# Strided sparse attention and an ELU layer: the first pair's q and k transposed as fp32, the first quarter of w_in in two loads, and a new order

## The chip, the cores and the metric

One core of a Trainium2 chip runs the whole program. The metric is the device time of one execution in microseconds. The engines are TensorE (PE; its weight loads are shown as PEld), VectorE (DVE), ScalarE (ACT), GpSimd (POOL) and SyncE (SP). Each takes its instructions in the order in which the program issues them and waits on semaphores for the others. Loads that also convert fp32 to bf16 are issued from POOL's queue; plain copies and stores from the queues of SP and ACT.

## The reference

Attention over 8 batches of 8 heads, 576 tokens of 64 features; heads 0 to 3 are local, heads 4 to 7 strided. Its result, 4608 tokens by 512 features, goes through two layers with an ELU between them.

```python
scores = scale * np.matmul(q, k.transpose(0, 1, 3, 2))
rel = pos[:, None] - pos[None, :]
mask_local = (rel >= 0) & (rel < stride)                      # stride = 32
mask_strided = (rel >= 0) & (pos[None, :] % stride == pos[:, None] % stride)
scores = np.where(masks, scores, -1e9)
attn = softmax(scores)
x = (attn @ v) as 4608 x 512
h = x @ w_in                                                  # 512 x 2048
g = np.where(h > 0.0, h, np.exp(np.minimum(h, 0.0)) - 1.0)
out = g @ w_out                                               # 2048 x 512
```

## The kernel before

Heads go in pairs. A key such as 0s1 names batch 0, strided heads, second pair; 0l0 the first local pair. A pair passes through these steps, each written as a token with a letter: T (transposes of q or k on PE, for batches 0 and 1 only; later batches use transposing DMAs, X), c or C (the copy of a transpose out of PSUM, on DVE or ACT), S (scores, L453), e (exponential on ACT, L460), m (mask on DVE, L467 and L473), O (the products with v and the row sums, L480 to L501), n and r (Ln and Exp, by which ACT takes the reciprocal of the sums, L551 and L556), x (the scaling on DVE that writes xT, L581). Most steps come in two halves.

The layers work on nine chunks of 512 tokens. The first layer makes 16 tiles of 128 hidden features for a chunk, four matmuls of 512 columns each (L608); two of the four read the strided half of xT, two the local half. For chunk 0 the halves are separate tokens, a (strided) and b (local); later chunks use L for all four. Then h (exponential, ACT), i or j (clamp on DVE, L625, or ACT, L623), g (maximum, DVE). The second layer, Z (L642), adds up 16 matmuls for each of four groups of 128 tokens; q or o copies the result out (L648, DVE or ACT) and t or u stores it. The last group is cut into pieces, Y and y (L672, L682).

The order of all this is written out by hand in the string ORDER, some 1400 tokens that are run one after another; a token's last digits name the PSUM banks. The order of one engine's instructions is that of the tokens. D tokens are loads on POOL's queue. W (L588) copies v of a strided batch into its layout, V (L585) moves rows of a local batch, and F fills constants. w tokens are filler: matmuls on a tile of zeros (L385) that write to a bank nobody reads yet.

The loads of POOL's queue share eight semaphores, so that the ninth in flight waits for the landing of the first.

For pair 0s0 the kernel doesn't use a converting load. Ahead of ORDER, SP loads q and ACT loads k of its two heads as fp32 into `stage`, each in two halves (L297). The tokens K and k cast the halves to bf16 (L390, on ACT or DVE), and T with a part number transposes four blocks of 72x128 (L401), whose copies are at L421. Heads 0s1 arrive as bf16 by two loads on POOL.

Of the kernel before, what the change touches and what calls it, by code (L numbers as in the profile page):

```python
# [8 lines left out]
F32 = mybir.dt.float32  # L9
BF16 = mybir.dt.bfloat16  # L10
I32 = mybir.dt.int32
ALU = mybir.AluOpType
# [35 lines left out]
C.1s0.q i.0.4 a.0.13.6 h.0.6 g.0.4 a.0.14.5 b.0.12 a.0.15.2 h.0.12 b.0.15 j.0.6 D.vs.1 a.0.2.1 j.0.12
b.0.13 g.0.6 b.0.2 h.0.13 g.0.12 a.0.1.4 h.0.2 i.0.7 b.0.1 i.0.13 a.0.3.3 g.0.7 h.0.1 D.wo3.0 b.0.3
i.0.2 b.0.14 h.0.3 g.0.2 a.0.0.7 j.0.1 b.0.0 a.0.11.1 g.0.1 h.0.0 a.0.10.0 h.0.14 D.vl.1 i.0.0 b.0.10  # L50
j.0.3 g.0.0 b.0.11 h.0.10 a.0.8.4 g.0.3 b.0.8 h.0.11 g.0.13 Z.0.0.0.7 h.0.15 i.0.10 D.ks.2 i.0.14
Z.0.0.1.7 h.0.8 g.0.10 j.0.11 Z.0.3.0.6 j.0.15 g.0.11 D.vs.2 Z.0.3.1.6 g.0.15 g.0.14 a.0.9.3 D.qs.2
i.0.8 b.0.9 g.0.8 Z.0.1.0.5 h.0.9 j.0.9 T.1s0.k.4 D.kl.2 Z.0.1.1.5 C.1s0.k g.0.9 T.1s1.k.2 S.1s0.1.01
c.1s1.k T.1l1.k.4 e.1s0.1 T.1l1.q.3 c.1l1.k T.1l0.q.2 S.1s1.0.01 m.1s0.1 Z.0.3.2.6 e.1s1.0 C.1l1.q
m.1s1.0 Z.0.1.2.5 C.1l0.q O.1s1.0.43 T.1l0.k.2 n.1s1.0 S.1s1.1.01 c.1l0.k Z.0.0.2.7 e.1s1.1 r.1s1.0
S.1s0.0.01 S.1l1.1.23 x.1s1.0 e.1s0.0 Z.0.1.3.5 m.1s1.1 m.1s0.0 e.1l1.1 Z.0.0.3.7 q.0.1 m.1l1.1 D.kl.3
S.1l0.1.01 S.1l1.0.23 V.1 e.1l0.1 Z.0.3.3.6 q.0.0 e.1l1.0 O.1l1.1.54 X.ks.2 m.1l1.0 O.1s0.1.73 n.1l1.1
m.1l0.1 S.1l0.0.01 n.1s0.1 Z.0.2.0.2 q.0.3 r.1l1.1 r.1s0.1 x.1l1.1 e.1l0.0 O.1s0.0.64 x.1s0.1 O.1l1.0.53
W.2 n.1s0.0 O.1l0.1.71 n.1l1.0 Z.0.2.1.2 m.1l0.0 r.1s0.0 X.qs.2 n.1l0.1 x.1s0.0 r.1l1.0 D.ql.2
O.1s1.1.04 r.1l0.1 x.1l1.0 O.1l0.0.63 n.1s1.1 x.1l0.1 Z.0.2.2.2 n.1l0.0 r.1s1.1 r.1l0.0 Z.0.2.3.2  # L60
x.1s1.1 X.kl.2 x.1l0.0 L.1.12.7 t.0.1 L.1.6.6 h.1.12 i.1.12 L.1.3.5 h.1.6 D.ks.3 i.1.6 L.1.4.4 h.1.3
D.vl.2 g.1.6 L.1.1.3 g.1.12 h.1.4 i.1.3 L.1.5.6 h.1.1 g.1.3 D.vs.3 L.1.13.7 i.1.4 h.1.5 i.1.1 i.1.5
L.1.0.5 h.1.13 g.1.5 D.qs.3 o.0.2 L.1.7.1 g.1.1 j.1.13 D.ql.3 g.1.4 h.1.0 L.1.2.6 X.ql.2 h.1.7 g.1.13
L.1.10.0 j.1.0 i.1.7 h.1.2 g.1.7 L.1.14.7 t.0.2 h.1.10 g.1.0 j.1.2 S.2s1.0.12 S.2s1.1.34 i.1.10 t.0.0
L.1.8.5 g.1.2 e.2s1.1 e.2s1.0 g.1.10 L.1.15.6 t.0.3 h.1.8 m.2s1.1 m.2s1.0 h.1.14 S.2s0.0.01 S.2s0.1.23
X.ks.3 L.1.9.4 e.2s0.1 i.1.14 g.1.14 h.1.15 L.1.11.3 e.2s0.0 i.1.15 h.1.9 Z.1.3.0.7 g.1.15 h.1.11 i.1.8
Z.1.3.1.7 j.1.9 g.1.8 m.2s0.1 O.2s1.1.01 Z.1.2.0.2 i.1.11 n.2s1.1 g.1.9 O.2s0.1.56 r.2s1.1 g.1.11
Z.1.2.1.2 n.2s0.1 x.2s1.1 Z.1.3.2.7 r.2s0.1 m.2s0.0 O.2s1.0.01 x.2s0.1 Z.1.2.2.2 n.2s1.0 O.2s0.0.34
r.2s1.0 Z.1.3.3.7 n.2s0.0 x.2s1.0 Z.1.2.3.2 r.2s0.0 q.1.3 S.2l0.0.01 S.2l0.1.56 x.2s0.0 Z.1.1.0.7
e.2l0.0 q.1.2 e.2l0.1 m.2l0.0 S.2l1.0.01 S.2l1.1.34 X.qs.3 Z.1.1.1.7 m.2l0.1 e.2l1.0 e.2l1.1 m.2l1.0  # L70
O.2l0.0.56 O.2l0.1.01 X.kl.3 n.2l0.0 m.2l1.1 Z.1.0.0.4 n.2l0.1 Z.1.0.1.4 r.2l0.0 t.1.3 O.2l1.1.23
r.2l0.1 x.2l0.0 Z.1.0.2.4 n.2l1.1 x.2l0.1 O.2l1.0.56 r.2l1.1 Z.1.0.3.4 X.ql.3 n.2l1.0 x.2l1.1 Z.1.1.2.7
r.2l1.0 D.qs.4 Z.1.1.3.7 x.2l1.0 D.kl.4 q.1.0 L.2.11.6 W.3 S.3s0.0.01 S.3s0.1.23 h.2.11 L.2.3.5 e.3s0.1
i.2.11 g.2.11 L.2.7.4 D.ks.4 h.2.3 o.1.1 D.vl.3 i.2.3 L.2.2.6 m.3s0.1 e.3s0.0 g.2.3 L.2.5.7 h.2.7 h.2.2
i.2.7 L.2.4.5 h.2.5 g.2.7 j.2.2 i.2.5 L.2.9.3 m.3s0.0 h.2.4 D.vs.4 g.2.5 L.2.0.4 h.2.9 g.2.2 j.2.4
D.ql.4 L.2.14.7 i.2.9 h.2.0 g.2.4 O.3s0.1.01 h.2.14 g.2.9 L.2.10.6 n.3s0.1 i.2.0 L.2.6.5 i.2.14 h.2.10
g.2.0 r.3s0.1 L.2.8.3 i.2.10 X.ks.4 g.2.14 h.2.6 L.2.13.4 x.3s0.1 h.2.8 j.2.6 g.2.10 O.3s0.0.01 X.qs.4
L.2.1.7 n.3s0.0 i.2.8 g.2.6 L.2.15.6 r.3s0.0 g.2.8 t.1.0 h.2.1 L.2.12.5 x.3s0.0 h.2.15 X.kl.4 i.2.1
S.3s1.0.01 S.3s1.1.23 g.2.1 e.3s1.1 Z.2.1.0.7 e.3s1.0 m.3s1.1 i.2.15 h.2.13 m.3s1.0 S.3l0.0.01
S.3l0.1.23 h.2.12 g.2.15 Z.2.1.1.7 e.3l0.1 i.2.12 j.2.13 Z.2.1.2.7 g.2.12 e.3l0.0 g.2.13 O.3s1.1.23  # L80
S.3l1.0.01 S.3l1.1.56 m.3l0.1 n.3s1.1 Z.2.1.3.7 m.3l0.0 e.3l1.1 Z.2.0.0.4 e.3l1.0 m.3l1.1 r.3s1.1
m.3l1.0 O.3s1.0.01 q.2.1 O.3l1.1.56 Z.2.0.1.4 n.3l1.1 x.3s1.1 t.2.1 n.3s1.0 Z.2.3.0.7 r.3l1.1 X.ql.4
O.3l1.0.23 Z.2.0.2.4 r.3s1.0 x.3l1.1 n.3l1.0 x.3s1.0 Z.2.3.1.7 t.1.2 r.3l1.0 S.4s1.0.01 S.4s1.1.56
x.3l1.0 t.1.1 Z.2.0.3.4 e.4s1.1 e.4s1.0 m.4s1.1 O.3l0.1.23 O.3l0.0.56 q.2.0 n.3l0.1 Z.2.3.2.7 W.4
r.3l0.1 Z.2.2.0.4 m.4s1.0 D.vs.5 n.3l0.0 x.3l0.1 O.4s1.1.01 D.ks.5 r.3l0.0 Z.2.2.1.4 D.vl.4 n.4s1.1
x.3l0.0 Z.2.3.3.7 r.4s1.1 L.3.14.6 x.4s1.1 D.qs.5 L.3.2.5 h.3.14 q.2.3 D.vl.5 i.3.14 S.4l0.0.01
S.4l0.1.23 h.3.2 L.3.7.7 g.3.14 e.4l0.0 i.3.2 e.4l0.1 L.3.11.6 D.kl.5 g.3.2 h.3.7 m.4l0.0 S.4s0.0.01
S.4s0.1.23 h.3.11 m.4l0.1 L.3.1.5 e.4s0.1 X.ks.5 e.4s0.0 Z.2.2.2.4 m.4s0.1 i.3.7 j.3.11 m.4s0.0
O.4s0.1.01 Z.2.2.3.4 g.3.11 n.4s0.1 g.3.7 O.4s0.0.23 r.4s0.1 L.3.0.6 n.4s0.0 x.4s0.1 D.ql.5 L.3.5.7
r.4s0.0 q.2.2 h.3.1 L.3.4.1 x.4s0.0 h.3.5 X.qs.5 L.3.6.4 j.3.1 i.3.5 h.3.0 g.3.5 L.3.15.0 h.3.6 g.3.1  # L90
t.2.0 h.3.4 L.3.12.7 i.3.0 h.3.15 g.3.0 t.2.2 L.3.3.5 j.3.4 i.3.6 h.3.12 g.3.4 L.3.8.6 h.3.3 g.3.6 j.3.3
O.4l0.1.12 i.3.12 L.3.10.3 n.4l0.1 g.3.3 L.3.9.4 i.3.15 h.3.8 g.3.15 h.3.10 L.3.13.5 g.3.12 r.4l0.1
h.3.9 Z.3.0.0.0 x.4l0.1 j.3.9 i.3.10 Z.3.2.0.7 D.qs.6 h.3.13 g.3.10 j.3.8 D.ks.6 Z.3.0.1.0 g.3.9 g.3.8
O.4l0.0.12 Z.3.2.1.7 i.3.13 n.4l0.0 X.kl.5 g.3.13 Z.3.0.2.0 r.4l0.0 x.4l0.0 S.5s0.0.34 S.5s0.1.56
Z.3.0.3.0 e.5s0.1 m.5s0.1 S.4l1.0.12 S.4l1.1.56 o.3.0 Z.3.2.2.7 e.4l1.1 e.4l1.0 Z.3.1.0.0 m.4l1.1 X.ql.5
# [638 lines left out]
```

## Time and profile before

| what | value |
|---|---|
| median of 3 runs | 306.0 us (305.95 to 306.1) |
| the profiled execution | 306.22 us |
| its span in the trace | 304.5 us |
| DMA engines, share over the first 36 us after 4.9 | 1.24 to 1.46, at 195 to 210 GB/s |
| first L608 (first layer) | 18.62 us |

The profile shows one execution. The span is the time between the first and the last recorded event; the execution took some 1.7 us more. Busy time of PE counts a matmul's whole passage: one of 512 columns is recorded as 379 ns, while the next starts 216 ns after it, so that small gaps don't show as idle. A timeline row gives start, length, engine, line, operation, output and input, shape, count, and in brackets the idle time before it and what ended it.

The granted PE clock is 1.00 in every stage that was looked at. The first eight filler matmuls nevertheless start 0.43 us apart, the later ones of the same size 0.216.

### The profile page before, as it was taken

The numbers are of one execution on the slowest core, as the hardware profiler recorded it, in microseconds if no ns is written. First come the engines' busy times: TensorE is split into PE (matmuls) and PEld (weight loads), VectorE is DVE, ScalarE is ACT, GpSimd is POOL, SyncE is SP. The second block draws the span as 40 slices with busy tenths as digits, with TensorE's granted clock in tenths as the row PEclk, the third lists the DMA queues.
The fourth block names the chain that finished last, engine by engine and source line by source line (L and its number), as shares of the span: only waits on it lengthen the run. The fifth ranks groups of instructions, "written<-read, shape, count | busy, mean of one in ns | idle before, by whom it ended". The sixth has DMA issues, their size and how long they took to land.

```text
span 304.5 us, 6258 instructions
## 1 busy us (share of the span) xinstructions
PE 297.1 (98%) x2339; PEld 146.8 (48%) x2339; DVE 226.2 (74%) x435; ACT 228.5 (75%) x412; POOL 80.2 (26%) x110
## 2 busy tenths in 40 slices
PE   6999999999999999999999999999999999999994
PEld 2654455445544454445544554445444544444444
DVE  6777968798779978896788878976788358895020
ACT  4778678598879888997989889978777559982101
POOL 8922436830471008530188250000000000000000
PEclk9999999999999999999999999999999999999999
DMA  8999999999899759999899499801120022000053
GB/s 165 190 206 207 207 193 169 169 198 204 158 158 168 128 123 134 162 192 171 196 154 154 61 132 149 195 16 56 38 69 0 2 69 69 2 1 0 4 155 119
DMA packets 107358, 37.63 MB, mean 124 GB/s; under 512 B 89152, under 2 KB 102848, under 8 KB 107328
## 3 DMA queue, kind: packets, MB, share of 16 engines
q0 software_dynamic: 69728, 19.47, 62.3%
q1 hardware_dynamic: 36920, 17.08, 28.4%
q10 hardware_dynamic: 680, 0.69, 0.8%
q8 instruction: 18, 0.29, 0.4%
q14 instruction: 12, 0.10, 0.1%
HBM read 39.53 MB, written 9.44 MB: 161 GB/s over the span
## 4 chain that ended last, share of the span: by engine, by line
PE 86%; DVE 6%; ACT 3%; issue 2%; DMA 2%; ACTq 0%; DVEq 0%
PE ps L642 40%; PE ps L608 33%; PE ps L453 4%; DVE g L636 3%; DVE he L625 2%; PE ps L523 2%; PE ps L516 2%; DMA g<-in_k_dram 2%; PE ps L385 1%; PE ps L672 1%; ACT he L616 1%; PE ps L411 1%; PE ps L496 1%; PE ps L480 1%; ACT ln L551 0%
## 5 line engine op out<-in xcount | busy, mean ns | idle before, releaser
L642 PE MATMUL ps<-w_out_sb,g 128*128 128x512 bf16 x560 | 132.8, 379 | 0.5 <-DVE g L636 0.5
L608 PE MATMUL ps<-xT,w_in_sb 128*128 128x512 bf16 x576 | 130.5, 379 | 0.2 <-DVE g L634 0.2
L616 ACT ACTIVATE he<-ps 128x512 f32<-128x512 f32 x144 | 80.9, 596 | 22.2 <-PE ps L608 20.0
L608 PEld LDWEIGHTS <-w_in_sb 128*128 128x128 bf16 x576 | 55.0, 98 | 64.3 <-issue 1.1
L642 PEld LDWEIGHTS <-g 128*128 128x128 bf16 x560 | 51.1, 98 | 55.7 <-issue 0.8
L636 DVE TENSOR_TENSOR g<-he,ps 128x512 bf16<-128x512 bf16 x92 | 62.0, 684 | 1.9
L581 DVE TENSOR_TENSOR xT<-ps,ln 64x576 bf16<-64x576 f32 (+1 forms) x64 | 42.6, 678 | 20.3 <-ACT ln L556 19.4
L460 ACT ACTIVATE e<-ps 72x576 bf16<-72x576 f32 (+1 forms) x64 | 39.1, 647 | 12.7 <-PE ps L453 11.9
L625 DVE TENSOR_SCALAR he<-he 128x512 bf16<-128x512 f32 x92 | 40.2, 446 | 7.5 <-ACT he L616 6.8
L551 ACT ACTIVATE ln<-ps 64x576 f32<-64x576 f32 (+1 forms) x64 | 36.3, 583 | 10.0 <-PE ps L523 5.0
L634 DVE SCALAR_TENSOR_TENSOR g<-he,ps 128x512 bf16<-128x512 bf16 x52 | 34.8, 682 | 7.2 <-ACT he L623 6.9
L556 ACT ACTIVATE ln<-ln 64x576 f32<-64x576 f32 (+1 forms) x64 | 38.5, 619 | 1.2
L623 ACT ACTIVATE he<-he 128x512 bf16<-128x512 f32 x52 | 32.5, 630 | 1.3 <-DVE g L636 0.8
L648 DVE COPY osb<-ps 128x512 f32<-128x512 f32 x22 | 15.1, 685 | 16.3 <-PE ps L642 16.0
L243 POOL DMA_DIRECT2D ql<-in_q_dram x24 | 20.1, 840 | 7.7 <-DMA vl<-in_v_dram 4.1
L648 ACT COPY osb<-ps 128x512 f32<-128x512 f32 x13 | 7.6, 586 | 17.9 <-PE ps L642 14.1
L250 POOL DMA_DIRECT2D kl<-in_k_dram x24 | 17.8, 747 | 11.4 <-DMA w_out_sb<-in_moe_w_out_dram 3.7
L473 DVE TENSOR_TENSOR pm<-e,mask_l 128x576 bf16<-128x576 bf16 x32 | 14.1, 453 | 6.9 <-ACT e L460 5.3
L467 DVE TENSOR_TENSOR pm<-e,mask_s 72x576 bf16<-72x576 bf16 x32 | 14.2, 451 | 4.3 <-ACT e L460 4.1
L260 POOL DMA_DIRECT2D vl<-in_v_dram x8 | 9.8, 1220 | 9.5 <-PE ps L523 7.2
L233 POOL DMA_DIRECT2D vs<-in_v_dram x8 | 5.2, 652 | 25.6 <-DVE vsp L588 24.7
L516 PEld LDWEIGHTS <-vsp 72*128 72x128 bf16 x192 | 9.1, 98 | 5.5 <-issue 0.4
(93 smaller groups left out, 153.2 us busy)
## 6 DMA issues: line engine op xcount, KB each, us to landing
out_dram<-osb SPq DMA_DIRECT2D x30, 144.0 KB
vl<-in_v_dram POOLq DMA_DIRECT2D x8, 288.0 KB, 8.9
w_in_sb<-in_moe_w_in_dram POOLq DMA_DIRECT2D x4, 512.0 KB, 13.1
w_out_sb<-in_moe_w_out_dram POOLq DMA_DIRECT2D x4, 512.0 KB, 16.8
kl<-in_k_dram POOLq DMA_DIRECT2D x24, 72.0 KB, 7.3
ql<-in_q_dram POOLq DMA_DIRECT2D x24, 72.0 KB, 8.4
ks<-in_k_dram POOLq DMA_DIRECT2D x5, 320.0 KB, 8.2
vs<-in_v_dram POOLq DMA_DIRECT2D x5, 320.0 KB, 9.1
```

What stands on the lines that cost most here:

```text
L460: nc.scalar.activation(e[0:R], tiles.pop(("S", key, u))[0:R], ACT.Exp, scale=scale)
L551: nc.scalar.activation(t, s_ps, ACT.Ln)
L556: nc.scalar.activation(t, t, ACT.Exp, scale=-1.0)
L581: nc.vector.tensor_mul(dst, o_ps, rc)
L608: nc.tensor.matmul(tiles["h", ch, m], lhsT=w_in_sb[:, c, m * 128:(m + 1) * 128], rhs=xT[:, c, ch * CHUNK:(ch + 1) * CHUNK], start=(c == 2) ...
L616: nc.scalar.activation(e, tiles["h", i[0], i[1]], ACT.Exp)
L623: nc.scalar.activation(e1, e, ACT.Relu, bias=1.0, scale=-1.0)
L625: eng.tensor_scalar(e1, e, scalar1=1.0, scalar2=1.0, op0=ALU.min, op1=ALU.subtract)
L634: nc.vector.scalar_tensor_tensor(dst, e1, -1.0, h, op0=ALU.mult, op1=ALU.max)
L636: nc.vector.tensor_tensor(dst, e1, h, op=ALU.max)
L642: nc.tensor.matmul(ops, lhsT=g[ch % 2][:, m, kk * 128:(kk + 1) * 128], rhs=w_out_sb[:, m, :], start=(m == 0), stop=(m == MC - 1), skip_gro ...
L648: eng(o_sb, tiles.pop(("o", int(ch), int(kk))))
```

## The change

The two fp32 halves of q and k of pair 0s0 are transposed as they are, against an fp32 identity, into fp32 PSUM; the casts to bf16 (tokens K and k, function `cast`) are gone, and the copies out of PSUM convert. The scores of 0s0 take 72 instead of 128 columns of k. The load of a quarter of w_in can be made in two parts, first the rows for the strided half of xT, then the others; it is done so for the last quarter, which is now the first to be used. ORDER is a new string throughout: the order of loads, of steps and of tiles, the banks, the split of clamps and copies between DVE and ACT, and the filler are all other than before.

```diff
+    identity_f = consts.tile([RS, RS], F32, tag="identity_f", name="identity_f")
...
+    nc.vector.memset(identity_f, 1.0)
+    nc.gpsimd.affine_select(
+        identity_f, identity_f, compare_op=ALU.is_equal, fill=0.0,
+        base=0, pattern=[[1, RS]], channel_multiplier=-1)
...
-            nc.gpsimd.dma_start(out=w_in_sb[:, :, i * 512:(i + 1) * 512],
-                                in_=w_in_v[:, :, i * 512:(i + 1) * 512])
+            cs = slice(0, KC) if y is None else (slice(2, KC), slice(0, 2))[int(y)]
+            nc.gpsimd.dma_start(out=w_in_sb[:, cs, i * 512:(i + 1) * 512],
+                                in_=w_in_v[:, cs, i * 512:(i + 1) * 512])
...
-    def cast(eng, nm, i):
-        n, f = "qk".index(nm), 2 * NS * D
-        eng(half(raw[nm + "s"][0:RS, 0:f], int(i)), half(stage[0:RS, n * f:(n + 1) * f], int(i)))
...
-        t = ps[:, bank, :].bitcast(BF16)[:, 0:S // (1 + len(part))]
+        t = ps[:, bank, 0:W] if part else ps[:, bank, :].bitcast(BF16)[:, 0:S]
...
         if part:
+            n = "qk".index(nm) * 2 * NS * D
+            src = stage[0:RS, n:n + 2 * NS * D].rearrange("p (h f) -> p h f", h=2)
             for i in range(NS // 2):
                 x, sp = divmod(i, NS // 4)
                 c0 = (NS // 2 * int(part[0]) + 2 * sp) * D
-                nc.tensor.transpose(t[:, i * RS:(i + 1) * RS], src[:, P.head(x), c0:c0 + 2 * D],
-                                    identity[0:RS, 0:RS])
+                nc.tensor.transpose(t[:, i * RS:(i + 1) * RS], src[:, x, c0:c0 + 2 * D], identity_f)
...
-                nc.tensor.matmul(dst, lhsT=P.kT[pr, k0:k0 + 128], rhs=rhs, start=True, stop=True,
+                n = RS if key == "0s0" else 128
+                nc.tensor.matmul(dst[0:n], lhsT=P.kT[pr, k0:k0 + n], rhs=rhs, start=True, stop=True,
                                  skip_group_check=True)
```

Parts of the two orders around their start and the first tiles of the first layer; first before, then after:

```
w.7.512.512.512.512.512.512.512.512 D.ql.0.1 F.vp D.kl.0.1 F.v1 D.ql.0.0 k.q.0 F.ms D.vs.0.0 T.0s0.q.0.7
D.kl.0.0 K.q.1 K.k.1 D.vs.0.1 K.k.0 C.0s0.q.0 w.0.512.512.512.512.512 T.0s0.k.0.6 D.vl.0 T.0s0.k.1.5
T.0s0.q.1.4 c.0s0.k.0 T.0s1.k.7 c.0s0.k.1 c.0s1.k w.0.324 T.0s1.q.6 c.0s0.q.1 D.wi1.0 S.0s0.0.01 c.0s1.q
...
w.2.224.224 O.0l0.0.10 n.0l1.1 x.0s0.1 r.0l1.0 w.1.142 O.0l0.1.54 r.0l1.1 x.0l1.0 D.ks.1 n.0l0.0
w.4.224.224 a.0.5.6 x.0l1.1 n.0l0.1 a.0.7.7 r.0l0.0 a.0.4.0 r.0l0.1 x.0l0.0 a.0.6.4 D.kl.1 x.0l0.1
T.1s1.q.3 b.0.5 c.1s1.q b.0.7 h.0.5 b.0.4 h.0.7 i.0.5 b.0.6 h.0.4 g.0.5 T.1s0.q.5 D.wo2.0 a.0.12.3
```

```
w.7.512.512.512.512.512.512.512.512 F.v1 D.kl.0.1 D.vs.0.0 F.vp D.ql.0.1 F.ms D.vs.0.1 T.0s0.q.0.7
D.kl.0.0 T.0s0.k.0.6 c.0s0.q.0 D.ql.0.0 c.0s0.k.0 w.0.512.512.172 T.0s0.k.1.7 S.0s0.0.01 C.0s0.k.1
T.0s0.q.1.6 e.0s0.0 D.vl.0 c.0s0.q.1 w.2.512.512.512 T.0s1.q.7 T.0s1.k.6 D.wi3.0.0 c.0s1.q S.0s0.1.01
C.0s1.k m.0s0.0 T.0l1.k.5 D.wi0.0 e.0s0.1 c.0l1.k w.2.403 S.0s1.1.67 S.0s1.0.23 D.wi3.0.1 e.0s1.1
...
F.ml S.0l0.1.23 e.0l1.0 D.ks.1 V.0 r.0s1.0 w.4.512.512 S.0l0.0.67 m.0l1.1 r.0s0.0 x.0s1.0 e.0l0.0
w.4.512 O.0l1.1.41 m.0l1.0 n.0l1.1 x.0s0.0 w.0.224.168 O.0l1.0.07 e.0l0.1 D.wo1.0 w.6.237 a.0.15.1
n.0l1.0 m.0l0.1 a.0.14.6 r.0l1.1 m.0l0.0 r.0l1.0 O.0l0.1.75 x.0l1.1 O.0l0.0.32 x.0l1.0 n.0l0.1 a.0.12.4
n.0l0.0 a.0.13.5 r.0l0.1 r.0l0.0 D.wo2.0 a.0.1.2 x.0l0.1 x.0l0.0 a.0.0.0 b.0.1 D.wo3.0 b.0.15 b.0.14
```

## The prediction

> **What bounds the kernel now.** I read the page's busy shares first, then TensorE's waits, then the timeline of the first 21 us, then the stages.
>
> ```profile
> span 304.5 us, 6258 instructions
> PE 297.1 (98%) x2339; PEld 146.8 (48%) x2339; DVE 226.2 (74%) x435; ACT 228.5 (75%) x412; POOL 80.2 (26%) x110
> ```
>
> ```profile
> PE ps L385 <- DVE zero L303: 1.3, 1, 1.3
> PE ps L401 <- ACT ks L390: 0.9, 1, 0.9
> PE ps L642 <- DVE g L636: 0.5, 1, 0.5
> PE ps L453 <- DVE qTs L421: 0.2, 1, 0.2
> PE ps L401 <- ACT qs L390: 0.2, 1, 0.2
> PE ps L608 <- DVE g L634: 0.2, 1, 0.2
> ```
>
> TensorE (PE) sets the end. It waits visibly for 3.3 us in all, and its largest wait after the start is 0.9 us for the ScalarE (ACT) cast of k. But the 98% hides the start: what PE does before the first L608 (the first layer) is partly filler on `zero` (L385), so a shorter start shortens the kernel.
>
> ```profile
> 4.28 0.62 ACT L390 CAST qs<-g 72x512 bf16<-72x512 f32 x1 [1.22 <-DMA g<-in_q_dram]
> 4.95 0.30 PE L401 MATMUL ps<-identity,qs 72*128 72x72 bf16 x4 [0.19 <-ACT qs L390]
> ...
> 6.07 1.14 ACT L390 CAST ks<-g 72x512 bf16<-72x512 f32 x2 [1.17 <-DMA g<-in_k_dram]
> ...
> 7.26 0.43 PE L401 MATMUL ps<-identity,ks 72*128 72x72 bf16 x8 [0.92 <-ACT ks L390]
> ...
> 8.41 0.30 PE L453 MATMUL ps<-qTs,kTs 64*128 64x72 bf16 x8
> ...
> 8.76 0.65 ACT L460 ACTIVATE e<-ps 72x576 bf16<-72x576 f32 x1 [1.26 <-PE ps L453]
> ...
> 18.62 1.89 PE L608 MATMUL ps<-xT,w_in_sb 128*128 128x512 bf16 x8
> ...
> 20.35 0.42 PE L408 MATMUL ps<-identity,xT 72*128 72x72 bf16 x8
> ...
> 20.75 1.89 PE L608 MATMUL ps<-xT,w_in_sb 128*128 128x512 bf16 x8
> ```
>
> The second half of k has landed at 6.0; the casts make 7.2 of it. First scores at 8.41, first exponential at 8.76. From there to the last reciprocal (L556) ACT runs until 20.03, about 11.3 us almost without a pause. The first layer splits there: tokens `a` (8 matmuls from 18.62) need only the strided heads, tokens `b` (from 20.75) need the last local head.
>
> **The change, part by part.**
>
> *Casts.* Gone are three ACT casts (0.62, 1.14 for two) and one VectorE (DVE) cast (0.42). The transposes now read the fp32 staging, landed at about 4.3 and 5.6 (q) and 4.6 and 6.0 (k). Filler ends at about 4.65 (eighth start 4.22, 0.43 apart).
>
> *fp32 transposes.* [...] Lower bound: 33 ns, the spacing of the bf16 ones in L401. Upper bound: one load (98 ns, the mean of the PEld rows at L401) and four streams of 33 ns, 0.23 us. I take load and one stream one after the other, 0.13 us, since that shape is nearest to L401. So a group of four takes 0.52 us against 0.13.
>
> *Their copies.* 288 columns now leave PSUM as f32. L421 took 0.30 us from bf16; from f32 I interpolate the DVE copies L682 (128 columns, 0.29) and L648 (512 columns, 0.685): 0.45, so 0.15 more for each of three on DVE. On ACT I take 0.40 (L421 there: 0.39). An identity of 72x72 adds about 0.1 us to DVE's fills and 0.3 to GpSimd (POOL) before its third load; that load had 4.8 us to land with others ahead of it in the queue, which hides 0.3.
>
> *The new start.* Two chains. DVE: the mask fill ends at 5.6, two f32 copies make 6.55, scores (0.25) 6.85, second q group 7.37. PE: 4.65 + two groups 1.04 + filler 1196 columns 0.50 + third group 0.52 + scores 0.25 + fourth group 0.52 = 7.48, the later. Then filler 1536 columns 0.64, the two bf16 transposes of pair 0s1 0.54, 0.15 until the last is out: ACT can copy k of 0s1 at 8.8. From there ACT has, at its spacing in back-to-back rows, two copies of 0.57, seven exponentials of 0.59, eight Ln of 0.36, eight reciprocals of 0.385: 11.2 us, until 20.0. In before ACT had eight exponentials and one copy from 8.76 on: 20.03. **So the end of the attention of batch 0 doesn't move**: what the casts give goes into fp32 transposes, f32 copies, and an ACT queue that is the same length from 8.8.
>
> *What does move: the order of the first layer.* `b` starts at about 20.7 in both. Before it, the new order does 12 `a` matmuls instead of 8 and one transpose group. The strided x are now all written by about 17.1 (DVE reaches the last of them after V.0, the vl copy, which starts near 14.7 instead of 15.67; vl is issued at 7.12 and takes 6.8 to land, so 13.9 allows it). PE then has 12 x 0.216 + two O of 0.39 = 3.4 us of work until 20.6. Gain: 4 x 0.216 = 0.86, less the transposes that are still to be done, 0.26: **-0.6 us**. What is late if this fails is `b`, and with it everything.
>
> *w_in.* In before the loads land at 17.6, 22.1, 24.3 and 26.8, with batch 1's q in between, at some 2.5 us for 512 KB. In the new order the half quarter for `a` follows vl and lands at about 15.8 (half of 13.9 to 17.6), the next quarter at 18.8, the second half near 20.1, then 22.7 and 25.2; the same bytes are in by 26.8. PE asks for them at about 17.2, 19.7, 21.1, 23.5 and 26.1. Every one has 0.8 us or more, so I cost the split at nothing; the cover is the `a` matmuls ahead. Without it, as with one 512 KB load at 17.6, `a` would start 0.4 us later. The split adds one POOL issue (0.77 us) on a queue that waits for landings anyway (2.9 us before xT, 4.2 before w_out).
>
> *Everything after.* The same matmuls in another order; filler falls from 12903 to 11786 columns, already inside the times above. Where does PE wait later?
>
> ```profile
> 60.00:80.00 20.00, 19.78 (x172) 9.69 (x171) 18.10 (x35) 17.25 (x31) 3.62 (x5) 1.00 1.47 202
> 80.00:120.00 40.00, 39.44 (x324) 19.66 (x321) 33.21 (x61) 34.54 (x61) 14.82 (x19) 1.00 1.08 137
> ```
>
> The first figure is the length, the next PE, then PEld, DVE, ACT. 0.78 us is idle here, almost all there is between 21 and 290. By the spacing of starts against columns the lost time is larger, 1.9 us, as a matmul shows as busy for 163 ns after the next could start. The large losses lie at 64, 98 to 102 and 154, in runs of first-layer tiles. Along the order I summed DVE's and ACT's work, less the time of PE's: in before the queue reaches 2.2 us (DVE) and 1.9 (ACT) near 98 and 2.0 (ACT) near 65. In the new order the peaks there are 1.9 for DVE and 1.6 for ACT; new is DVE 1.7 near 161. Clamps on DVE rise from 92 to 103 (0.36 each) and output copies fall from 22 to 18 (0.62): +1.5 us on an engine at 74%; ACT loses 3.8. I take **-0.2 us**, between -1.9 (no loss left) and +2 (twice the loss). The last pieces (L672, L682, their stores) are alike.
>
> **Sum.** -0.6 - 0.2 = -0.8: a span of 303.7 for 304.5. The profiled execution took 306.22 for it, 0.22 above the median of 306.0, so the median becomes 305.2.
>
> **Rivals.**
>
> *A transpose of fp32 makes four passes (slower).* Then a group takes 4 x 0.23 = 0.92, and the PE chain, with 16 of them in it, is 16 x 0.10 = 1.6 us later; copy of 0s1, ACT's whole queue and `b` follow one for one. It decides from 0.17 us each on, where the 0.6 is used up. -0.8 + 1.6: 306.8. For it: no fp32 matmul is in this trace, and PE has only 1.1 us of filler on that stretch. Against: a transpose multiplies by ones, so parts of a number need not be crossed. The Trainium skill, FP8 and Floating Point Precision, TensorE Precision Notes, states four passes for true FP32; it does not say that a transpose pays them, and no run here has shown it.
>
> *The lead is given back.* ACT's queue has no air from 8.8 to 20.0; each wait in it delays `b`. DVE writes the mask, V.0 and five products between 14 and 17, and 0.5 us of delay there is likely enough; or batch 1's last x arrives late at the first tile of chunk 1 (ACT's queue there peaks at 2.6, against 2.1 in before). Then 305.8, no change.
>
> *The middle stalls more.* At 161 DVE has 11.3 us of work in 10.1 of PE, against 9.5 in 10.5; and DVE's vsp copy (L588) waits for v of batch 2, whose load is now behind q and k of that batch: 52 instead of 48.4 for a copy due near 54. With 1.5 us lost there: 306.9. Against: the sums of queues above are mostly shorter.
>
> *More gain:* 0.033 us per transpose takes another 0.4 off the start, and the stalls at 64 and 101 vanish: 304.3.
>
> **How the numbers follow.** Forecast 0.45 (own range 304.7 to 305.6), lead given back 0.18, four passes 0.17, middle 0.12, more gain 0.08. A measurement here tells about 0.2%, 0.6 us, from no change. Faster by more takes the forecast, less its upper edge, and the larger gain: 0.50. Same: 0.18 and some edges of its neighbours: 0.19. Slower: 0.31. The range goes from 304.2 to 307.1, where four passes and the middle end.
>
> **What would show it.** Right: no L390 rows; a transpose group of some 0.5 us at 4.7; first exponential near 7.2; ACT without idle from 8.8 to 20; 12 L608 before the first wait on xT, `b` at 20.7 or earlier; idle of PE in 60 to 120 below 0.78. Wrong: transposes over 0.17 us apart, `b` after 21.3, a first-layer matmul that waits for a w_in load, or idle of PE above 2 us after 21.

## The result and the profile after

The changed kernel takes 308.0 us (median of seven runs, 306.56 to 308.37), the kernel before 305.95 on the same chip (seven runs, 305.54 to 306.83): slower by 0.57% (ratio 1.0057, 95% interval 1.0035 to 1.0078). A second series gave 308.57 (six runs, 307.14 to 310.45; ratio 1.0091, 1.0061 to 1.012). The prediction was 305.2, with a range to 307.1. Medians and ranges below are over all runs of a kernel, while ratios leave out disturbed runs.

The profiled execution took 308.0 us, its span 306.3. First its head:

```profile
span 306.3 us, 6207 instructions
...
PE 293.8 (96%) x2294; PEld 147.6 (48%) x2333; DVE 224.1 (73%) x442; ACT 223.3 (73%) x402; POOL 81.0 (26%) x112
```

PE's waits, in all, how many, and the longest:

```profile
PE ps L499 <- DVE pm L476: 1.7, 1, 1.7
PE ps L456 <- DMA kTs<-ks: 1.7, 1, 1.7
PE ps L390 <- DVE zero L304: 1.3, 1, 1.3
```

The third was there before (as L385). The other two are new, and they are the two places where time goes. The timeline shows what each ends with; the lines are 3 higher than in the kernel before (L608 is L611, L585 is L588, L453 is L456).

```profile
4.64 1.17 PE L404 MATMUL ps<-identity_f,g 72*128 72x72 f32 x8
...
5.47 0.45 DVE L423 CAST qTs<-ps 128x288 bf16<-128x288 f32 x1
...
6.87 0.40 ACT L423 CAST kTs<-ps 128x288 bf16<-128x288 f32 x1 [3.82 <-PE ps L404]
...
7.04 1.18 POOL L260 DMA_DIRECT2D vl<-in_v_dram  x1
7.16 0.65 ACT L463 ACTIVATE e<-ps 72x576 bf16<-72x576 f32 x1
...
8.70 0.64 ACT L429 COPY kTs<-ps 128x576 bf16<-128x576 bf16 x1 [0.89 <-PE ps L410]
...
16.07 0.55 DVE L588 COPY vl<-vl 32x1472 bf16<-32x1472 bf16 x1 [1.78 <-DMA vl<-in_v_dram]
16.66 0.46 DVE L476 TENSOR_TENSOR pm<-e,mask_l 128x576 bf16<-128x576 bf16 x1
...
17.17 0.31 PE L499 MATMUL ps<-pm,ones 128*64 128x288 bf16 x2 [1.74 <-DVE pm L476]
...
17.21 0.65 ACT L463 ACTIVATE e<-ps 128x576 bf16<-128x576 f32 x1 [1.79 <-DVE pm L476]
...
18.39 0.81 PE L611 MATMUL ps<-xT,w_in_sb 128*128 128x512 bf16 x3
...
63.11 0.43 PE L456 MATMUL ps<-qTs,kTs 64*128 64x72 bf16 x16 [1.72 <-DMA kTs<-ks]
```

Up to 8.70 all is as predicted. Then V.0 (L588) waits on DVE for vl, which lands at 16.05, 9.0 us after its issue; in the kernel before it landed at 13.97. Behind V.0 in DVE's queue stands the mask product (L476), and for that wait O on PE and the next exponential on ACT: one late load stops three engines for about 1.75 us. The first L611 comes at 18.39 for 18.62 before, but with the wait inside it the kernel is 0.1 to 0.3 us behind at 22 (by the layers' matmuls alone, or by all but filler and transposes), where it should have been 0.6 ahead. The second loss is at 61.4: the scores of 2s1 need the transposing DMA of ks of batch 2. The chain of waits has both, start, length and what:

```profile
7.04 9.01 DMA vl<-in_v_dram
...
50.91 12.16 DMA kTs<-ks
```

In the kernel before, V.0, the issue of that transposing DMA, and the scores that need it:

```profile
15.67 0.55 DVE L585 COPY vl<-vl 32x1472 bf16<-32x1472 bf16 x1
...
46.98 2.00 SPq L601 DMA_TRANSPOSE kTs<-ks  x1
...
64.49 0.44 PE L453 MATMUL ps<-qTs,kTs 64*128 64x72 bf16 x16
```

Counted in weight loads of the two layers, the changed kernel is 0.4 us behind at 56 and 60, 2.35 at 64, 1.8 to 1.9 from 72 to 80 and 2.05 at 290; the last matmul starts at 302.45 for 300.40. The stage with the second wait, in the columns shown above for the kernel before:

```profile
60.00:80.00 20.00, 18.18 (x148) 8.73 (x149) 16.04 (x31) 16.56 (x30) 7.93 (x10) 1.00 1.53 160
80.00:120.00 40.00, 39.09 (x321) 19.70 (x326) 32.59 (x60) 34.40 (x60) 16.39 (x22) 1.00 1.39 161
```

PE idles 1.82 us from 60 to 80 (0.22 before) and 0.91 from 80 to 120 (0.56 before).

### The profile page after: what moved, and what is told of

Same layout as the page of the kernel before. It is cut to its first block, busy times and chain, and to the rows that moved or that the text cites. A ratio compares the mean times of both kernels' runs of the same rounds, so it can differ in the third digit from the quotient of the medians.

```text
span 306.3 us, 6207 instructions
## 1 busy us (share of the span) xinstructions
PE 293.8 (96%) x2294; PEld 147.6 (48%) x2333; DVE 224.1 (73%) x442; ACT 223.3 (73%) x402; POOL 81.0 (26%) x112
## 3 DMA queue, kind: packets, MB, share of 16 engines
q1 hardware_dynamic: 36836, 16.93, 31.2%
## 4 chain that ended last, share of the span: by engine, by line
PE 73%; DMA 12%; DVE 6%; POOL 3%; issue 3%; ACT 3%; POOLq 0%; ACTq 0%
PE ps L645 34%; PE ps L611 31%; DMA vl<-in_v_dram 8%; DMA kTs<-ks 4%; PE ps L456 3%; DVE g L639 2%; PE ps L526 2%; DVE he L628 2%; PE ps L519 1%; PE ps L675 1%; ACT he L619 1%; DVE xT L584 1%; POOL vs L233 1%; DVE g L637 1%; ACT e L463 1%
## 5 line engine op out<-in xcount | busy, mean ns | idle before, releaser
L645 PE MATMUL ps<-w_out_sb,g 128*128 128x512 bf16 x541 | 130.7, 379 | 1.3 <-issue 0.6
L611 PE MATMUL ps<-xT,w_in_sb 128*128 128x512 bf16 x558 | 129.5, 379 | 1.5 <-issue 0.3
L611 PEld LDWEIGHTS <-w_in_sb 128*128 128x128 bf16 x576 | 55.0, 98 | 64.2 <-issue 0.7
L639 DVE TENSOR_TENSOR g<-he,ps 128x512 bf16<-128x512 bf16 x103 | 68.4, 682 | 1.6
L628 DVE TENSOR_SCALAR he<-he 128x512 bf16<-128x512 f32 x103 | 43.7, 437 | 12.6 <-ACT he L619 11.9
L637 DVE SCALAR_TENSOR_TENSOR g<-he,ps 128x512 bf16<-128x512 bf16 x41 | 27.5, 681 | 5.2 <-ACT he L626 5.1
L626 ACT ACTIVATE he<-he 128x512 bf16<-128x512 f32 x41 | 25.4, 630 | 1.8 <-DVE g L639 1.1
L651 ACT COPY osb<-ps 128x512 f32<-128x512 f32 x17 | 9.9, 583 | 17.3 <-PE ps L645 12.6
L651 DVE COPY osb<-ps 128x512 f32<-128x512 f32 x18 | 12.3, 686 | 13.5 <-PE ps L645 12.3
L476 DVE TENSOR_TENSOR pm<-e,mask_l 128x576 bf16<-128x576 bf16 x32 | 14.2, 455 | 7.7 <-ACT e L463 6.8
L233 POOL DMA_DIRECT2D ks<-in_k_dram x7 | 4.6, 663 | 30.0 <-DMA kTs<-ks 28.1
## 6 DMA issues: line engine op xcount, KB each, us to landing
vl<-in_v_dram POOLq DMA_DIRECT2D x8, 288.0 KB, 12.9
```

The lines of the kernel that those rows point to most:

```text
L611: nc.tensor.matmul(tiles["h", ch, m], lhsT=w_in_sb[:, c, m * 128:(m + 1) * 128], rhs=xT[:, c, ch * CHUNK:(ch + 1) * CHUNK], start=(c == 2) ...
L626: nc.scalar.activation(e1, e, ACT.Relu, bias=1.0, scale=-1.0)
L628: eng.tensor_scalar(e1, e, scalar1=1.0, scalar2=1.0, op0=ALU.min, op1=ALU.subtract)
L637: nc.vector.scalar_tensor_tensor(dst, e1, -1.0, h, op0=ALU.mult, op1=ALU.max)
L639: nc.vector.tensor_tensor(dst, e1, h, op=ALU.max)
L645: nc.tensor.matmul(ops, lhsT=g[ch % 2][:, m, kk * 128:(kk + 1) * 128], rhs=w_out_sb[:, m, :], start=(m == 0), stop=(m == MC - 1), skip_gro ...
```

## The experiments

All kernels of one series were timed beside the kernel before on their own chip (305.7 to 305.95).

### First series: parts of the change one by one

**The change again.** Its timing is above.

> The changed kernel once more. Theory (two transfers decide: the local v of batch 0, and k of batch 2 through its transposing DMA): again VectorE waits over 1 us for the local v near 15 us, and the first scores of 2s1 wait over 1.2 us for the transposed k near 62 us; 307.5 to 308.3 us. Rival (one bad execution was profiled): one of the two waits is below 0.5 us, and the time stays at 307.5 to 308.3 with the loss somewhere else.

The profile has the same two waits, 2.4 us at L499 (vl lands at 16.79) and 0.9 at L456, the second shorter than the 1.2 expected. So the late vl is no accident of one execution.

**w_in's last quarter in one load**

```diff
-D.wi3.0.0
+D.wi3.0
...
-D.wi3.0.1
```

> The changed kernel with the last quarter of w_in loaded whole in the place of its first half, as the other quarters. If the instruction fetch of TensorE (16 KB at 14.5 us on one DMA engine, 1.27 us) makes the local v late, nothing changes there: it lands at 15.5 to 16.1, the first layer starts 0.2 to 0.6 us later, 308.0 to 308.6. If the half load itself does (its first packets took 0.25 to 0.42 us instead of 0.09, from 13.4 to 14.5 us), v lands near 14 and the time falls by 0.8 to 1.3 us.

307.43 us (306.54 to 309.9; ratio 1.0048, 1.0033 to 1.0063); vl lands at 15.90. The split load is not what delays vl; the time lies between the two that were forecast.

**Stores of chunk 0 later**

```diff
-t.0.3
...
-t.0.0
...
-X.ql.2
+X.ql.2 t.0.3 t.0.0
```

> The changed kernel with the stores of chunk 0's third and fourth result (512 KB) moved in the SP queue behind the four transposing DMAs of batch 2. If the stores take the DMA engines from the transposed k, it lands by 60 us, the wait of the scores of 2s1 (1.7 us) goes, and the time falls by 1.0 to 1.5 us, as the next limit is close. If the loads do, or the transfer itself, k lands at 62 or later and the time stays within 0.3 us.

306.94 us (304.84 to 309.42; ratio 1.0038, 1.0014 to 1.0062). kTs still lands at 62.24 and PE waits 1.0 us, though no store is under way until 64. The median is 1.1 and 1.6 us below the changed kernel's in its two series, as much as the theory of the stores had it, but the landing moved by only 0.8 us and the intervals of the ratios overlap; what the stores are worth isn't shown.

**fp32 transposes in the old order**

```diff
-k.q.0
-K.q.1 K.k.1
-K.k.0
+    identity_f = consts.tile([RS, RS], F32, tag="identity_f", name="identity_f")
...
+                nc.tensor.transpose(t[:, i * RS:(i + 1) * RS], src[:, x, c0:c0 + 2 * D], identity_f)
```

> The kernel before, in its old order, with fp32 transposes in place of casts and bf16 transposes, and nothing else. Theory: the casts stood in ScalarE's idle time ahead of a queue that ends at 20 us either way, and the new copies take 0.15 us more each, so within 0.3 us of before (305.7 to 306.3). Rival (the casts are the price of the start): first exponential 0.8 us or more earlier, time lower by 0.5 to 1.0.

306.42 us (306.23 to 308.73; ratio 1.0027, 1.0011 to 1.0043): slower than before although its first exponential is earlier, 8.45 for 8.76. The order is the old one, yet vl lands at 16.04:

```profile
16.06 0.55 DVE L591 COPY vl<-vl 32x1472 bf16<-32x1472 bf16 x1 [0.54 <-DMA vl<-in_v_dram]
...
19.02 1.24 PE L614 MATMUL ps<-xT,w_in_sb 128*128 128x512 bf16 x4
```

In before that copy starts at 15.67 without a wait and the first layer at 18.62. So what makes vl late came with the fp32 transposes or with what was added for them, not with the order.

### Second series: is it the transposes, and what the waits cost

**The kernel before, profiled again**

> The kernel before, unchanged, profiled once more. In its first profile vl landed at 13.97 us, 6.9 us after its issue; in each of the five profiles with fp32 transposes it landed between 15.48 and 16.79. Theory A (the late landing belongs to the kernels with fp32 transposes): vl again at 13.8 to 14.2, V.0 without a wait, span near 304.5. Theory B (the landing varies from execution to execution, and the first profile of before was a lucky one): vl at 15 or later, V.0 waits, the first L608 some 0.4 us later and the span near 305.

305.57 us, span 303.9; vl lands at 14.20 and V.0 doesn't wait. Theory A, as far as two profiles tell.

**Casts in the new order**

```diff
+k.q.0 T.0s0.q.0.7
...
+K.k.0 T.0s0.k.0.6
...
+K.q.1
...
+K.k.1 T.0s0.k.1.7
...
-    identity_f = consts.tile([RS, RS], F32, tag="identity_f", name="identity_f")
```

> The changed kernel with the casts of before put back (two of k and one of q on ScalarE, one on VectorE, bf16 transposes), in the new order. Theory A (fp32 transposes make vl late): vl lands by 14.2 and the time falls to about 306.3, though ScalarE has 1.8 us more ahead of its exponentials. Theory B (vl is late whatever the transposes read): vl at 15.3 or later, V.0 waits as in the changed kernel; the first exponential goes from 7.16 to about 8.2, and as ScalarE waits 1.8 us for the mask product behind V.0 anyway, the time stays within 0.5 us of the changed kernel's 307.5 to 308.5.

vl lands at 14.14: theory A, as far as vl goes. The time was forecast by neither: 306.9 us, but five of the twelve executions take 304.25 to 305.34, four 309.04 to 309.8 and three lie between (ratio 0.9998, 0.9977 to 1.0019). The profiled execution, 309.04, is one of the four; its filler of 512 columns, three in a row, and later:

```profile
7.85 1.48 PE L385 MATMUL ps<-zero 128*128 128x512 bf16 x3
...
17.56 1.10 PE L385 MATMUL ps<-zero 128*128 128x224 bf16 x5
...
20.46 0.39 PE L385 MATMUL ps<-zero 128*128 128x512 bf16 x1
...
21.91 1.03 PE L609 MATMUL ps<-xT,w_in_sb 128*128 128x512 bf16 x4
```

Three such matmuls took 0.81 us at 7.33 in the changed kernel, here 1.48; the five of 224 columns 0.65 at 13.10, here 1.10. PE stays at half rate until 20.35 (the trace's record of the granted clock), and the first layer starts 3.3 us late. That the short executions are those in which PE gets its full rate early is likely; none of them was profiled.

**V.0 moved behind two strided products**

```diff
-V.0 r.0s1.0
+r.0s1.0
...
-r.0s0.0 x.0s1.0
+r.0s0.0 x.0s1.0 V.0
```

> The changed kernel with V.0, the copy of vl on VectorE, behind the first mask product of the last local pairs and two strided products instead of ahead of them. Theory (V.0 at the head of VectorE's queue is what turns a late vl into a late start): ScalarE's 1.8 us wait on the mask product goes, the strided products are written 1.8 us earlier, the first O of local heads follows vl by 0.6 instead of 1.1 us; tokens b start 0.8 to 1.2 us earlier and the time falls to about 306.8. Rival (what is late is the O that reads vl itself, not the queue): the start moves by at most 0.5 us and the time stays at 307.3 or above.

307.86 us (307.39 to 310.66; ratio 1.008, 1.0049 to 1.0112): the time was a miss. The start did gain: PE waits 0.8 us there for 1.7, and at 56 it is 0.5 us ahead of the changed kernel. But the lead only makes the next wait longer. PE's waits, and windows (length, then busy time of PE, PEld, DVE, ACT and POOL, the granted clock, DMA share and GB/s):

```profile
PE ps L456 <- DMA kTs<-ks: 2.8, 1, 2.8
...
PE ps L504 <- DVE vl L588: 0.8, 1, 0.8
```

```profile
24.00:60.00 36.00, 35.09 (x351) 18.03 (x356) 28.52 (x59) 26.26 (x54) 11.32 (x16) 1.00 1.55 178
60.00:66.00 6.00, 3.24 (x26) 1.26 (x25) 3.83 (x8) 2.54 (x6) 1.78 (x3) 0.85 1.28 150
66.00:70.00 4.00, 3.95 (x29) 1.68 (x29) 1.85 (x4) 2.56 (x5) 4.00 (x6) 0.80 1.24 218
```

After the wait of 2.76 us the windows show a granted clock of 0.85 and 0.80: half rate for 3.41 us, from 64.16 to 67.57. This wait is paid twice: once as idle time, and once by the matmuls after it at half rate.

**Loads of ql of batch 2 behind the load of qs of batch 3**

```diff
-D.ql.2
...
-D.qs.3
+D.qs.3 D.ql.2
```

> The changed kernel with the four loads of ql of batch 2 behind the load of qs of batch 3 in GpSimd's queue, which waits for the first transposing DMA; so they no longer run beside the transposing DMA of ks of batch 2. Theory (that DMA is late because ordinary loads share the DMA engines with it): kTs lands at 58 to 60 instead of 63.07, TensorE's wait of 1.7 us near 61.4 goes, and the time falls by 1 to 1.8 us, to about 306.5; the spread of its runs shrinks. Rival (it is late because of the stores of chunk 0 and the transposing DMAs' own length): kTs still lands after 61.5 and the time stays within 0.5 us of the changed kernel, or rises if ql of batch 2 is now late for scores near 80.

307.37 us (306.56 to 308.7; ratio 1.0053, 1.0034 to 1.0071). kTs lands at 57.60, 6.2 us after its issue for 12.2, and the wait at L456 is gone; the profiled execution is 306.56. The mechanism is right: ordinary loads running beside it draw the transposing DMA out; in the two other profiles with these loads moved, below, it takes 7.5 and 7.2 us. The median gained less than expected, as the scores of the local heads now wait 0.4 us for ql at 77, and the start is as late as before.

### Third and fourth series: the tile

What do the kernels with a late vl share, if not the order? All have `identity_f`. It is 72 fp32 columns, 288 bytes a partition, and stands ahead of nearly all the tiles that loads write. If tiles lie in the order in which they are allocated (the trace shows no addresses), it moves them by 288 bytes.

**The tile last, and 512 bytes wide**, so that the tiles ahead of it lie as before:

```diff
-    identity_f = consts.tile([RS, RS], F32, tag="identity_f", name="identity_f")
...
     mask_l = consts.tile([128, 2, NS, 3, LN], BF16, tag="mask_l", name="mask_l")
+    identity_f = consts.tile([RS, 128], F32, tag="identity_f", name="identity_f")[:, 0:RS]
```

> The changed kernel with its fp32 identity (72 columns, 288 bytes a partition) moved behind all other constant tiles and widened to 512 bytes, so that the tiles which loads write keep the addresses that they have in the kernel before. So far vl landed at 13.97 to 14.20 us in the three profiles without this tile (two of before, one of the new order with casts) and at 15.48 to 16.79 in the seven with it. Theory P (the tile's 288 bytes shift the raw tiles, vl and osb to addresses at which the DMA engines write more slowly): vl at 13.9 to 14.3, under 10 packets of 1 KB over 0.2 us between 8 and 18 us, no wait of V.0, the transposing DMA of ks of batch 2 lands at 58 to 60.5, and the time falls by 1.5 us or more, to 305.5 to 306.3. Rival (it is the fp32 transposes themselves, or what TensorE does meanwhile): vl still at 15.3 or later and the time stays within 0.6 us of the changed kernel's 307.3 to 308.5.

> The order of before with fp32 transposes in place of the casts, and the fp32 identity placed last and widened as in the run beside it. Theory P: packets of 128 bytes take 33 ns on the mean as in before (40.8 with the tile in the middle), vl lands by 14.3, and what is left is the worth of the transposes without casts in the old order: first exponential at 8.45 for 8.76, so 305.3 to 305.8, against 306.4 with the tile in the middle. Rival: vl at 15.3 or later, 306.2 or above.

In the new order: 305.64 us (304.98 to 308.27, twelve runs; ratio 1.0004, 0.9983 to 1.0026), 2.4 us below the first series of the changed kernel by one line. In the old order: 305.73 (305.32 to 306.73; ratio 1.0, 0.999 to 1.001) for 306.42. PE's longer waits in the first of them, and its stage of batch 2:

```profile
PE ps L499 <- DVE pm L476: 1.4, 1, 1.4
PE ps L390 <- DVE zero L304: 1.3, 1, 1.3
PE ps L645 <- issue: 0.6, 4, 0.2
```

```profile
60.00:80.00 20.00, 19.84 (x170) 9.65 (x171) 17.39 (x33) 18.10 (x32) 11.08 (x14) 1.00 1.64 172
```

kTs lands at 60.59, and the scores go at 61.12 without a wait; idle from 60 to 80 falls from 1.82 to 0.16 us. In these two profiles the kernel with the tile last is ahead of the changed one by 0.2 to 0.3 us at 22 and 60 and by 2.0 at 64, so there the tile's price is above all the wait for ks. On vl theory P missed: its last part lands at 15.65, and at 15.34 in the old order, and V.0 still waits, 1.21 us in the new order and 0.15 in the old:

```profile
15.67 0.55 DVE L588 COPY vl<-vl 32x1472 bf16<-32x1472 bf16 x1 [1.21 <-DMA vl<-in_v_dram]
```

**The kernel before with an unused tile of that size, and nothing else**

```diff
+    spare = consts.tile([RS, RS], F32, tag="spare", name="spare")
     ones = consts.tile([128, D], BF16, tag="ones", name="ones")
...
+    nc.vector.memset(spare[:, 0:1], 0.0)
```

> The kernel before with one unused tile of 72 fp32 columns (288 bytes a partition) where the change puts its fp32 identity, and nothing else changed but one memset of a single column. Theory P (addresses): vl at 15.3 or later, over 40 packets of 1 KB above 0.2 us between 8 and 18 us, packets of 128 bytes over 35 ns on the mean, and the time rises by 0.4 to 1.5 us to 306.2 to 307.3. Rival (the placement matters only together with fp32 transposes or the new order): vl by 14.3 and 305.8 as before.

306.54 us (306.34 to 307.22, five runs; ratio 1.0031, 1.0019 to 1.0043). No fp32 transposes, no new order, only a tile: 0.8 us. Its copy of vl now waits, though it starts only 0.1 us later than the 15.67 of before.

```profile
15.78 0.55 DVE L587 COPY vl<-vl 32x1472 bf16<-32x1472 bf16 x1 [0.31 <-DMA vl<-in_v_dram]
```

Its first layer starts at 18.74 for 18.62, and from 22 to 60 it isn't behind the kernel before; the transposing DMA of ks of batch 2 takes 7.4 us for 7.8. Where the 0.8 us goes was not located.

**The tile where the change put it, at other widths**

```diff
+    identity_f = consts.tile([RS, 80], F32, tag="identity_f", name="identity_f")[:, 0:RS]
```

> The changed kernel with its fp32 identity where the change put it, but 80 columns wide (320 bytes, a multiple of 64 but not of 128). If whole multiples of 64 bytes are enough: 305.4 to 306.2 as with the tile placed last, few slow packets. If 128 bytes or more are needed: 307.3 to 308.5 as the changed kernel, vl at 15.3 or later with over 40 slow packets.

> The same with 128 columns (512 bytes): every later tile moves by 512 bytes instead of 288. If the remainder of the address decides: 305.4 to 306.2, few slow packets. Rival (any move of those tiles costs, or what helped was only that the tile came last): 307.3 or above.

With 80 columns (320 bytes) 307.93 us (306.78 to 309.76; ratio 1.0078, 1.0054 to 1.0103), as slow as with 288. With 128 columns (512 bytes) 306.05 (304.88 to 308.42; ratio 1.0011, 0.9993 to 1.0029). So it is not that the tiles move, nor that the identity came last, but by how much they move: a multiple of 64 bytes is not enough, one of 512 is.

Counted from the packets of each trace: vl's 16 landings (the 15th and the last), packets of 1 KB that took more than 0.2 us between 8 and 18 us, and the mean of the 50,496 packets of 128 bytes:

```
kernel                        bytes   15th   last   slow 1 KB   128 B, ns
before                            0  13.90  13.97       1         32.9
before again                      0  13.98  14.20       3         32.9
casts in the new order            0  14.01  14.14       4         34.9
before, spare tile              288  15.02  15.76      48         39.1
changed kernel                  288  15.32  16.05      51         35.8
changed kernel again            288  15.72  16.79      43         38.7
fp32, old order                 288  15.92  16.04      69         40.8
changed, 80 columns             320  15.47  15.88      32         35.1
changed, 128 columns            512  14.31  16.94      10         33.9
changed, tile last             last  14.21  15.65       4         34.2
fp32, old order, tile last     last  14.33  15.34       4         33.4
```

The slow packets split cleanly by the tile: 10 at most where nothing, 512 bytes or a last tile is added, 32 or more with 288 or 320 bytes. So they do in the profiles that the table leaves out: 43 to 74 in the five other kernels with the 288 bytes in the middle, 4 to 6 in the four others with the tile last. The 15th landing follows with one exception: up to 14.41 without the shift, 15.02 or later with it, but 15.14 in one profile with the tile last (nine fillers, V.0 moved, 6 slow packets). The mean of the 128-byte packets leans the same way, less cleanly. The last landing, for which V.0 waits, does not split so: in all seven profiles with fp32 transposes and the tile mended, one of the 16 comes 0.4 to 2.6 us after the 15th, and the last lands between 14.67 and 16.94, in four of them at 15.6 or later, as with the tile in the middle (15.47 to 16.79). The kernels without fp32 transposes and without the tile have no such late part. In each of the seven a 16 KB instruction fetch begins between 13.1 and 14.1 and takes 0.97 to 0.99 us. That the fetch goes through the late engine is possible, but the trace names no engine, it wasn't tried by moving the fetch, and in the two profiles of before a fetch begins at 13.79 and 13.88, when vl is nearly in, without a late part. That the fp32 transposes themselves delay this last part isn't excluded.

**Nine fillers instead of eight, tile last**

```diff
-w.7.512.512.512.512.512.512.512.512
+w.7.512.512.512.512.512.512.512.512.512
```

> The changed kernel with the identity placed last, and a ninth filler matmul of 512 columns at the start. Fillers of 512 columns are 0.43 us apart until about 5.0 us in before, until 5.4 to 7.8 us in the kernels that turn to fp32 transposes after eight fillers, and 0.21 afterwards. Theory G (TensorE gets its full rate after some 3.8 us of unbroken matmuls, and transposes do not count towards it): fillers after the first group at 0.21 in the profile, the transposes 0.06 instead of 0.12 apart, first exponential at 7.0 to 7.3, and the runs at 308 that the placed-last kernel had twice in twelve vanish; median 305.0 to 305.7. Rival (0.43 us later, nothing gained): first exponential at 7.4 or later, 305.9 or above.

305.73 us (304.63 to 307.03; ratio 1.0, 0.9987 to 1.0013). Theory G falls: the transposes after nine fillers still start 0.120 us apart until 5.9. In another profile with nine fillers (V.0 moved, tile last) the full rate came during the eighth, at 4.1. By the traces' records of the granted clock it comes between 4.1 and 7.3 us with fp32 transposes, at 4.5 in the two profiles of before, at 6.9 with the spare tile and at 20.4 with casts in the new order, the last two with bf16 transposes; by what rule stays open. The two runs at 308 are gone, but two of twelve are too few to tell.

### Both waits removed

**The two moves together, without and with the tile last**

> The changed kernel with both moves that were tried singly: V.0 behind two strided products, and the loads of ql of batch 2 behind the load of qs of batch 3; the fp32 identity where the change put it. Theory (two separate losses, which add): the profile of V.0 moved led by 0.6 us at 56, that of the loads moved by 1.5 us from 64 on; together 2.1 us off a profiled span of 306.3: a span near 304.2 and a median of 305.5 to 306.3. Rival (moving one wait only brings up the next): 306.8 or above, with a new wait of TensorE over 1 us between 15 and 80.

> All three together: the fp32 identity placed last, V.0 moved, the loads of ql of batch 2 moved. Theory P: 304.3 to 305.3, below the kernel before. Rival (placement does nothing): as the run with the two moves alone, within 0.5 us of it.

307.64 us (305.61 to 310.04; ratio 1.0062, 1.0033 to 1.009) without. Neither of the two waits is over 1 us any more, and the profiled span of 304.5 is near the 304.2 expected, but the median is not: most runs are 1 to 4 us longer. With the tile last 305.83 (305.25 to 310.37; ratio 0.9999, 0.9989 to 1.0008), above the 304.3 to 305.3 expected. Placement, not order, steadies the runs. The mean granted clock of each execution shows it too: in the new order 25 of 62 executions with 288 or 320 bytes in the middle have 0.992 to 0.994, as in the profile of V.0 moved, whose half rate was 3.41 us long, but only 4 of 68 with the tile last or 512 bytes wide. How much of the time that is wasn't separated.

**Tile last, nine fillers, V.0 moved; and the stores moved too**

> Identity placed last, ninth filler, and V.0 behind two strided products: what singly helped the start or cost nothing. Theory (V.0's place is worth the 0.4 to 0.6 us that VectorE still waits for vl when an instruction fetch of TensorE falls into that load): 304.8 to 305.5, under the kernel before by 0.1 to 0.3%. Rival (the start's gain is lost at the scores of batch 2, which wait for the transposing DMA of ks all the longer, 0.8 us in the run with nine fillers): 305.6 to 306.2.

> The same with the stores of chunk 0 behind the last transposing DMA of batch 2. If the wait for ks of batch 2 takes what the start gained: 0.3 to 0.8 us below the run beside it, 304.6 to 305.2. If the loads of ql and not the stores delay that DMA: the same as the run beside it, within 0.3 us.

305.77 us (305.08 to 306.57; ratio 1.0001, 0.999 to 1.0012) and 305.53 (304.87 to 308.26; ratio 0.9996, 0.9979 to 1.0013): the first at the rival's number, the second within 0.3 us of it, so nothing shows that the stores delay that DMA. No version is measurably faster than the kernel before. The profiled execution of the last is one of its two long ones, 308.26:

```profile
17.55 0.32 PE L504 MATMUL ps<-pm,vl 128*64 128x96 bf16 x6 [1.57 <-DVE vl L588]
```

```profile
13.00:17.00 4.00, 2.79 (x53) 1.61 (x50) 2.47 (x9) 3.57 (x10) 1.35 (x3) 1.00 1.30 190
17.00:20.00 3.00, 2.44 (x21) 1.06 (x21) 2.56 (x7) 1.61 (x4) 1.40 (x2) 0.81 1.24 206
20.00:22.00 2.00, 2.00 (x19) 1.14 (x19) 0.45 (x2) 1.31 (x4) 0.74 (x1) 0.50 1.24 208
22.00:26.00 4.00, 3.95 (x18) 1.82 (x18) 1.54 (x5) 1.65 (x5) 1.39 (x2) 0.97 1.24 206
```

vl's last part landed at 16.93, PE waited 1.57 us, and the granted clock went to 0.50: half rate from 18.86 to 22.27. The other long one, 307.85, has the same mean clock, 0.993, where the nine short ones have 0.997 or more. The two at 308 of the kernel with the tile last have 1.00, so theirs is another cause, which wasn't seen.

## Why the prediction was wrong

- **The casts, the transposes and the copies: right.** Estimated 0.13 us a transpose between 0.033 and 0.23; measured 0.120 while PE is at half rate and 0.062 at full rate. The f32 copies took 0.45 on DVE and 0.40 on ACT, as estimated, the first exponential came at 7.16 ("near 7.2"), ACT's copy of 0s1 at 8.70 (8.8). Their loads were mis-sized, without harm: each of the 16 has a weight-load row (PEld at L404) of 0.14 to 0.23 us, where the estimate took 0.098.
- **w_in at nothing: right.** Its five loads landed at 17.30, 19.84, 21.12, 23.68 and 26.22, 1.0 to 1.5 us later than forecast, behind the late vl; no matmul of the first layer shows a wait for them. There is little to spare: with the tile last, the weight loads at L611 wait 0.9 us for them in all.
- **The rival of four passes: fell.** Full-rate fp32 transposes are 0.062 us apart, bf16 ones 0.033, so at most twice; its break-even was 0.17. The Trainium skill's four passes (FP8 and Floating Point Precision, TensorE Precision Notes) are not seen for a transpose.
- **The identity: mis-costed, and the largest loss of time.** The working has "An identity of 72x72 adds about 0.1 us to DVE's fills and 0.3 to GpSimd (POOL) before its third load". Its real price is the 288 bytes by which it moves the tiles behind it: 0.8 us for the old kernel, 2.4 for the changed one by the medians (1.6 to 2.7 by the ratios). No row of a profile of before could show that, and the list of costs had no place for it: a tile was costed by the work that fills it.
- **The step that failed first** is "vl is issued at 7.12 and takes 6.8 to land, so 13.9 allows it". The issue was at 7.04, the landing took 9.0. A duration under full DMA load was carried over unchanged. With it the -0.6 of the start became +0.1 to +0.3. The tile is not the whole of it: with the tile mended the landing still took 7.6 to 9.9 us in seven profiles, by its last part, and why that part is late stays open.
- **The middle, -0.2: wrong in its working too.** I summed the queues of DVE and ACT against PE and watched one late transfer, the copy for 52; the transfer that came to bind was the transposing DMA of ks of batch 2. In before it was issued at 46.98 and landed at 54.76, for scores at 64.49: 9.7 us of cover. In the new order q goes first, so ks is issued at 50.91, and the scores are due at 61.4. That left no room for 12.2 us. Even with the tile last the cover is 0.5 us (60.59 to 61.12), and with nine fillers PE waits 0.8 us there.
- **The rivals.** "The middle stalls more" had the size (1.5 us) and the sign, at another place and by another engine. With the tile mended, the profiled span of 303.3 is within 0.4 us of the 303.7 forecast, which is partly luck, as V.0 still waits 1.21 us in it; and the median (305.64) is the number of "lead given back", 305.8. Why the -0.8 is not there with the tile mended stays open: what makes most runs 0.6 us longer than that profiled one wasn't seen; in the long run of the last version the last part of vl was late.

What stays open besides: which remainder of an address is the bad one (only sums of 0, 288, 320 and 512 bytes were tried, and that tiles lie in the order of their allocation is assumed), and what sets the moment of PE's full rate. The Trainium skill (DMA: Bandwidth & Descriptors, How a descriptor splits into AXI transactions) states that a descriptor which doesn't start at a multiple of 256 bytes begins its first transaction at the multiple below, and that the bytes fetched ahead of its start are unused and still cost beats, of 32 bytes each. That fits which widths hurt, if the tiles lay at such multiples before, as 288 and 320 leave a remainder and 512 none. It is stated of what a transaction reads, though, and these are writes; and here the median packet of 128 bytes stays at 32 ns in every kernel while only the tail grows, which the rule doesn't tell.

## What to carry to other kernels

A new constant tile is an edit to every tile allocated after it: put it last, or round its bytes a partition up (512 was safe here, 320 not), before you judge what the change is worth. When an order is made anew, list every transfer with its landing and its first use, transposing DMAs included, and take cover of under 1 us under full DMA load as none. And moving work ahead of a wait that stays only lengthens that wait.

## What the runs showed of the hardware

- PE's clock can fall to half after a wait of 1.6 to 2.8 us. In three profiles the granted clock is 0.50 for 3.41 us: from 64.16 after a wait of 2.76 us (V.0 moved), from 64.72 after 2.46 (w_in in one load), and from 18.86 after 1.57 among small matmuls (the last version). After 2.38 us (the changed kernel again) and 2.48 (128 columns), both near 18, and after the two of 1.7 in the changed kernel it stayed at 1.00. So the length of a wait alone doesn't decide. The Trainium skill (TensorE: Matmul & The Clock Gate, HAM oscillation) warns of idle gaps over some 3.4 us; these three falls came after shorter ones.
- The transposing DMA of ks of batch 2 took 6.2 to 13.9 us from issue to landing, by what ran beside it. The tile's share in that is less clear: in the new order, with ql loaded beside it, 11.6 to 13.9 with 288 or 320 bytes in the middle, 10.1 to 12.0 with the tile mended, 12.9 with casts and no tile; in the old order 7.4 to 8.2 with and without.
- Instructions are fetched in packets of 16 KB on one queue, 18 in the changed kernel, each 0.9 to 2.8 us long over all profiles, the first after the start at 12.8 to 15.2. They are put down to PE, which has by far the most rows; the trace doesn't name the engine.
